# Four plain fp32 weight tiles instead of six, signs partly on ScalarE, quarter steps and a new instruction order in a fused RWKV and MLP kernel

## The chip, the cores and the metric

The kernel runs on one core of a Trainium2 chip. The metric is the device time of one execution in microseconds (us), and for a kernel it is the median of its runs.

The engines are named as in the profile. PE is TensorE's matmul unit and PEld its weight load, DVE is VectorE, ACT is ScalarE, POOL is GpSimd and SP is SyncE. Each engine takes its instructions in the order in which the program lists them for it.

## The reference

An RWKV recurrence over 768 time steps (4 batches, 8 heads of 48) gives `y`. The 3072 tokens of `y` then go through a two-layer MLP: 384 to 2048, an ELU, and back to 384.

```python
for t in range(S):
    kt, vt, rt, wt = (k[:, :, t], v[:, :, t], r[:, :, t], w[:, :, t])
    cur = np.einsum('bhd,bhe->bhde', u[None] * kt, vt)
    y[:, :, t] = np.einsum('bhd,bhde->bhe', rt, state + cur)
    state = wt[:, :, :, None] * state + np.einsum('bhd,bhe->bhde', kt, vt)
...
h = x @ w_in
g = np.where(h > 0.0, h, alpha * (np.exp(np.minimum(h, 0.0)) - 1.0))
return (g @ w_out).astype(np.float32)
```

The two weight matrices arrive as raw 64-bit floats, so the kernel builds fp32 values out of their two 32-bit words by itself.

## The kernel before

**Units and blocks.** The recurrence is cut into 24 units. Four units give the 512 tokens (columns) of one of six blocks. In the first block (block 0) a unit is 128 time steps of one batch, and so a quarter of the block's columns. The steps of a unit have short names:

- `es`, `gs`: two scans of the decays on DVE (L436, L446). `rh` multiplies keys and receptances by them (L451). `rkc` is a product for the diagonal (L470), which PE sums (`pd`, L475), ACT copies (`md`, L479) and ACT, DVE or POOL spreads (`sp`).
- `s`: PE transposes the keys and makes the scores (L516, L528). `mk`: DVE masks them (L540 in block 0, L542 later). `kt`: ACT copies the transposed keys (L546).
- `v`: PE multiplies by the values (L503, L568). `xf`, `xh`, `xl`: ACT and DVE move the result to SBUF, in block 0 as plain fp32 (`xf`), and as a rounded high part and the rest (`xh`, `xl`).

**MLP steps.** A block's MLP goes over 16 weight tiles f of 128 hidden units. One step has the first layer on PE (`g1`, L259 or L263), two activations on ACT (`r1` at L267, `r2` at L270), a combination on DVE (`stt`, L273), a rounding copy on ACT (`gh`, L277), the rest on DVE (`gl`, L281), and the second layer on PE (`g2`, L291 or L294). The result of `g1` lies in one of two PSUM tiles `ph`, which `stt` sets free. The second layer of a block adds up in three PSUM banks `acc`.

In the split form each product is three fp32r matmuls (high by high, high by low, low by high), so a step over 512 columns is 9 matmuls on PE. Six weight tiles (0 to 5) are used in block 0 as plain fp32 (L259, L291): 3 matmuls, each of which the program issues as two passes, and no `gh` and `gl`. In block 0 these six tiles are taken in halves of 256 columns: first the six first halves, which need units 0 and 1 only, then the six second halves. That makes 12 half steps and 10 full steps, numbered 0 to 21.

**Weights.** A tile comes in with one load of 768 KB (`raw`, L606, on SP). ACT scales the high word (`a`, L611), ACT or DVE shifts the low word (`cs`, L616 or L618), DVE joins them (`cb`, L626) and puts the sign in (`cc`, L630). For a split tile ACT then makes the high part (`wh`, L633) and DVE the low one (`wl`, L645). Tiles 0 to 5 are split after block 0 is through with them (`wt` L637 on ACT, `wl` on DVE, `wh` L641 on POOL). There is another branch: ACT writes the sign as a 16-bit float into the low word (`sg`, L622), and then one DVE operation (that of L626) does what `cb` and `cc` do. No tile uses it before the change. Tiles come through four staging buffers at first and two later, so that a later load waits until the `cc` of an earlier tile is done.

**The order.** All these steps are tasks of a planner (`Plan`, L100). It has a table of costs and due times, and plays the schedule through on paper. The instructions are then issued in the order that comes out. `NUDGE` (L87) moves the due times of single tasks by hand, and `FILL` (L45) puts matmuls on ones (L410) ahead of single PE steps. Those compute nothing that is used.

**The end.** In the last block the third bank's columns are finished in two parts (`end`, L303): columns 0 to 383 from PSUM tile `pa`, and columns 384 to 511 from `pb`. Three stores are issued by SP and one, of 128 columns, by ACT.

Of the kernel before, what the change touches and what calls it, by code (L numbers as in the profile page):

```python
# [8 lines left out]
F32 = mybir.dt.float32  # L9
# [11 lines left out]
P = 128  # L21
C = 128
# [5 lines left out]
N = B * C  # L28
# [5 lines left out]
WKR = dict(w=(0, W1), k=(W1, W1 + K1 + R1))  # L34
NU = NC * B
STEP = B // 2
FH = (6, 0)
WU = 64
CUT = 384
K32 = 6  # L40
SIGN_ACT = ()
LOW = ['DVE']*2+['ACT']*14
RAWS = ["raw0", "raw1", "x1a", "x1b"] * 2 + ["raw0", "raw1"] * 4
DUE = {0: 9.0}
FILL = {("pd", 0): 15, ("s", 0): 6, ("v", 0): 1, ("pd", 1): 4, ("v", 1): 1, ("pd", 2): 3, ("s", 2): 2, ("g1", 0): 6}  # L45


def _pieces():
    res = []
    for h in range(H):  # L50
        s, e = h * D, (h + 1) * D
        while s < e:
# [31 lines left out]

LEADS = dict(ld="ld_w ld_k ld_v ld_rk ld_wx", es="es gs", rh="rkc rh kh pc sc", sp="rk rku md pd sp", fl="fl", s="s mk kt", v="v xf xh xl up", raw="raw", a="a",
             cc="cand cs cb cc cx sg", wl="wh wl wt", g1="g1 r1 r2 stt", g2="g2 gh gl")
NUDGE = dict(cc={0: 5, 2: 19.5, 4: 15.75, 5: -13.25, 14: 4.25},  # L87
             es={3: 11.5, 5: -23.75, 7: 1, 11: -42.5, 17: -5.25, 20: 12.75, 21: 40.5},
             g1={16: -3.5, 19: -3.5, 20: 4.25, 23: 5.75, 29: -7.5, 30: -8.25, 31: -13.25, 33: 21, 38: -15.75, 40: -29.75, 42: -33.75, 44: -17.5, 48: -70.75, 51: 26.75, 55: 44, 56: -10.5, 58: -10, 68: 34, 82: -8, 83: 12.5, 84: 6, 93: -7.5},
             g2={2: 6.75, 3: 26.5, 10: 1.5, 19: -1.75, 25: 0.25, 27: 2.25, 30: 0.75, 31: 14.75, 32: -6.5, 35: 9, 37: -11.25, 43: 28.5, 46: -25.25, 51: 8.5, 58: -13, 64: 2.25, 65: 14.5, 71: -25.5, 85: 6.5, 93: 1.75},  # L90
             ld={2: -16, 13: -16.5, 21: -36.75},
             raw={0: -6.75, 1: -6},
             rh={1: 10.25, 4: -3.75, 9: -18.75, 14: 23.5, 16: -14},
             s={4: -29.75, 9: -2.25, 12: -30.25, 13: 5, 21: 8.5},
             sp={4: -19.25, 5: 8.75, 9: 39.5, 13: 29.5, 17: -6.5},
             v={2: -5.5, 15: -2, 17: 6.75, 18: 24, 20: 22.25})
KIND = {n: k for k, v in LEADS.items() for n in v.split()}


class Plan:  # L100
# [5 lines left out]
    def add(self, key, eng, dur, fn, after=(), due=None, start=0.0, lock=False, size=0):  # L106
        self.tasks[key] = dict(key=key, eng=eng, dur=dur, fn=fn, after=list(after), due=due, start=start, lock=lock, size=size,
                               nudge=NUDGE.get(KIND.get(key[0]), {}).get(key[1] if len(key) > 1 else 0, 0.0))

# [124 lines left out]
def mlp(nc, w_h, w_l, ps_acc, ps_h, ml, gp, po, dst, last=False, w_f=()):  # L234
# [61 lines left out]
    box = {}  # L296
# [4 lines left out]
        nc.scalar.copy(box["o"][:, m], acc[m])  # L301

    def end(m, cols=(0, N), rest=None):  # L303
        t = po.tile([P, cols[1] - cols[0]], F32, tag=("wraw", "wraw1", "wg")[m], name="o", bufs=m or 1)
        if rest is not None:
            nc.vector.tensor_tensor(t, rest, box["part"][:, cols[0]:cols[1]], ALU.add)
        else:
            (nc.vector.tensor_copy if m else nc.scalar.copy)(t, acc[m])
        (nc.scalar if cols[1] == N and m == 2 else nc.sync).dma_start(dst[m * P:(m + 1) * P, cols[0]:cols[1]], t)

    def partial():
        box["part"] = gp.tile([P, N], F32, tag="x2", name="part", bufs=1)
# [9 lines left out]
def rwkv_elu_kernel(ctx, tc, wkr, rk, vp, u, uz, gkrw, gv, gu, wraw, out):  # L322
    nc = tc.nc
# [10 lines left out]
    ld = pool("ld", 3)  # L334
# [300 lines left out]
    def conv_t(f):  # L635
        raws[f] = w_f[f], stg.tile([P, 2, NK, P], F32R, tag="wg", name="wt", bufs=SLOTS["wg"])
        nc.scalar.copy(raws[f][1], w_f[f])  # L637
# [24 lines left out]
    add, hold, K = plan.add, plan.hold, COST  # L662
    steps = []
    for c in range(NC):
        fh = FH[c] if c < len(FH) else 0
        fs = list(range(NF)) if c == 0 else list(range(K32, NF)) + list(range(K32))
        steps.append([(f, 0, N // 2) for f in fs[:fh]] + [(f, N // 2, N) for f in fs[:fh]] + [(f, 0, N) for f in fs[fh:]])

    add(("const",), "POOL", 0.5, constants)
    add(("ubd",), "SP", DMA_ISSUE, lambda: load_u(True), due=7.0, size=4.0)  # L670
# [1 line left out]
    for u_ in units:  # L672
        i, c = u_["i"], u_["c"]
# [51 lines left out]
    for f in range(NF):  # L725
        add(("raw", f), "SP", DMA_ISSUE, lambda f=f: load_w(f), start=RAW_AT[min(f, 1)], size=694)
        add(("a", f), "ACT", K["a"], lambda f=f: conv_a(f), [("raw", f)])
        e = LOW[f]
        add(("cs", f), e, K["la" if e == "ACT" else "cand"], lambda f=f: conv_low(f), [("raw", f)], lock=e == "DVE")
        if f in SIGN_ACT:  # L730
            add(("sg", f), "ACT", K["sg"], lambda f=f: conv_sign(f), [("cs", f)])
            add(("cc", f), "DVE", K["cv"], lambda f=f: conv_b(f), [("sg", f), ("a", f)], lock=True)
        else:
            add(("cb", f), "DVE", K["cv"], lambda f=f: conv_b(f), [("cs", f), ("a", f)], lock=True)
            add(("cc", f), "DVE", K["cv"], lambda f=f: conv_c(f), [("cb", f)], lock=True)
        if f >= K32:
            add(("wh", f), "ACT", K["wh"], lambda f=f: conv_h(f), [("cc", f)])
            add(("wl", f), "DVE", K["wl"], lambda f=f: conv_l(f), [("wh", f)], lock=True)
        else:
            add(("wt", f), "ACT", K["wh"], lambda f=f: conv_t(f), [("g2", f), ("g2", f + FH[0])])  # L740
            add(("wl", f), "DVE", K["wl"], lambda f=f: conv_l(f), [("wt", f)], lock=True)
            add(("wh", f), "POOL", K["wg"], lambda f=f: conv_m(f), [("wl", f)], lock=True)
    prior = None
# [4 lines left out]
    for c in range(NC):  # L748
        fns = mlp(nc, w_h, w_l, ps_acc, ps_h, ml, gp, stg, out[:, c * N:(c + 1) * N], last=c == NC - 1, w_f=() if c else w_f)
        t = BEGINS[c]  # L750
# [225 lines left out]
```

## Time and profile before

| | |
|---|---|
| median of 3 runs | 513.03 us (511.89 to 513.47) |
| the profiled execution's own time | 512.88 us |
| its span | 510.8 us |
| PE busy | 498.9 us, 98% of the span |
| DVE busy | 336.5 us, 66% |
| ACT busy | 270.7 us, 53% |
| POOL busy | 94.8 us, 19% |
| HBM read and written | 45.42 MB and 4.72 MB |

A profile row gives an engine, a line, an operation, the tiles written and read, a count, and times. Busy times of PE are modelled and overlap, so what one matmul costs in a stream is the distance between starts. The chain of work that ended last shows that distance: its pieces are start, length and what ran. In the timeline a row is start, length, instruction, and in brackets the idle time just ahead of it with the engine that ended it. "DVE m L273" is `stt`, and "DVE am L542" is `mk`.

### The profile page before, as it was taken

The numbers are of one execution on the slowest core, as the hardware profiler recorded it, in microseconds if no ns is written. First come the engines' busy times: TensorE is split into PE (matmuls) and PEld (weight loads), VectorE is DVE, ScalarE is ACT, GpSimd is POOL, SyncE is SP. The second block draws the span as 40 slices with busy tenths as digits, with TensorE's granted clock in tenths as the row PEclk, the third lists the DMA queues.
The fourth block names the chain that finished last, engine by engine and source line by source line (L and its number), as shares of the span: only waits on it lengthen the run. The fifth ranks groups of instructions, "written<-read, shape, count | busy, mean of one in ns | idle before, by whom it ended". The sixth has DMA issues, their size and how long they took to land.

```text
span 510.8 us, 13742 instructions
## 1 busy us (share of the span) xinstructions
PE 498.9 (98%) x6000; PEld 409.6 (80%) x6000; DVE 336.5 (66%) x469; ACT 270.7 (53%) x520; POOL 94.8 (19%) x94
## 2 busy tenths in 40 slices
PE   8999999999999999999999999999999999999994
PEld 8887778778888888887888888888888877888883
DVE  7999999997799433598633588734499543324232
ACT  4988475757545255565735554343555344534451
POOL 2001124004373100542100271400161100000000
PEclk9999999999999999999999999999999999999998
DMA  8958926302931001944200854204312000000001
GB/s 277 353 192 274 268 93 181 97 4 74 276 91 50 3 1 42 293 137 109 57 3 3 267 161 124 72 1 117 113 50 76 3 3 3 34 27 1 0 2 67
DMA packets 18882, 51.09 MB, mean 100 GB/s; under 512 B 2304, under 2 KB 2688, under 8 KB 18816
## 3 DMA queue, kind: packets, MB, share of 16 engines
q1 hardware_dynamic: 18672, 50.08, 32.2%
q8 instruction: 49, 0.80, 0.7%
q14 instruction: 17, 0.14, 0.1%
q10 hardware_dynamic: 144, 0.07, 0.0%
HBM read 45.42 MB, written 4.72 MB: 98 GB/s over the span
## 4 chain that ended last, share of the span: by engine, by line
PE 84%; DVE 5%; ACT 5%; DMA 3%; issue 1%; DVEq 0%; SPq 0%; ACTq 0%
PE acc L294 35%; PE ph L263 34%; PE pa L503 6%; DMA wraw<-in_wraw_dram 3%; PE pa L528 2%; PE pa L568 2%; PE pb L516 1%; PE ph L259 1%; ACT wraw L616 1%; PE acc L291 1%; DVE wg L626 1%; ACT m L270 1%; PE acc L410 1%; DVE m L273 1%; ACT m L267 1%
## 5 line engine op out<-in xcount | busy, mean ns | idle before, releaser
L273 DVE SCALAR_TENSOR_TENSOR m<-m,ph 128x512 f32<-128x512 f32 (+1 forms) x102 | 66.3, 651 | 96.6 <-ACT m L270 96.4
L267 ACT ACTIVATE m<-ph 128x512 f32<-128x512 f32 (+1 forms) x102 | 58.3, 571 | 108.4 <-PE ph L263 98.0
L263 PE MATMUL ph<-xh,w_l 128*128 128x512 f32 x270 | 105.5, 391 | 0.0
L294 PE MATMUL acc<-gh,w_l 128*128 128x512 f32 x268 | 104.7, 391 | 0.0
L281 DVE TENSOR_TENSOR gl<-m,gh 128x512 fp32r<-128x512 f32 x90 | 64.9, 723 | 38.7 <-ACT gh L277 38.4
L277 ACT CAST gh<-m 128x512 fp32r<-128x512 f32 x90 | 55.7, 619 | 58.4 <-PE acc L294 30.3
L294 PE MATMUL acc<-gh,w_h 128*128 128x512 f32 x180 | 72.0, 400 | 0.0
L263 PE MATMUL ph<-xh,w_h 128*128 128x512 f32 x180 | 71.7, 398 | 0.0
L294 PE MATMUL acc<-gl,w_h 128*128 128x512 f32 x180 | 70.4, 391 | 0.0
L263 PE MATMUL ph<-xl,w_h 128*128 128x512 f32 x180 | 70.2, 390 | 0.0
L270 ACT ACTIVATE m<-m 128x512 f32<-128x512 f32 (+1 forms) x102 | 61.8, 606 | 2.2
L263 PEld LDWEIGHTS ph<-xh,w_l 128*128 128x128 f32 x270 | 50.7, 188 | 10.9
L294 PEld LDWEIGHTS acc<-gh,w_l 128*128 128x128 f32 x268 | 50.3, 188 | 10.6
L496 POOL TENSOR_SCALAR_AFFINE_SELECT am<-md 64x512 f32<-64x512 f32 x32 | 28.9, 903 | 115.6 <-DVE md L465 58.6
L458 POOL TENSOR_TENSOR rk<-rk 128x384 f32<-128x384 f32 x20 | 26.4, 1321 | 120.6 <-DMA rk<-in_rk_dram 120.2
L294 PEld LDWEIGHTS acc<-gh,w_h 128*128 128x128 f32 x180 | 33.8, 188 | 7.8
L263 PEld LDWEIGHTS ph<-xh,w_h 128*128 128x128 f32 x180 | 33.8, 188 | 7.8 <-DVE m L273 0.5
L294 PEld LDWEIGHTS acc<-gl,w_h 128*128 128x128 f32 x180 | 33.8, 188 | 6.8 <-DVE gl L281 0.2
L263 PEld LDWEIGHTS ph<-xl,w_h 128*128 128x128 f32 x180 | 33.8, 188 | 6.7
L263 PE MATMUL ph<-xh,w_g 128*128 128x512 f32 x90 | 36.4, 404 | 0.0
L263 PE MATMUL ph<-xl,w_g 128*128 128x512 f32 x90 | 35.2, 391 | 0.0
L294 PE MATMUL acc<-gh,w_g 128*128 128x512 f32 x88 | 34.9, 397 | 0.0
(116 smaller groups left out, 738.6 us busy)
## 6 DMA issues: line engine op xcount, KB each, us to landing
wraw<-in_wraw_dram SPq DMA_DIRECT2D x16, 768.0 KB, 6.0
k<-in_wkr_dram SPq DMA_DIRECT2D x24, 448.0 KB, 7.0
rk<-in_rk_dram SPq DMA_DIRECT2D x20, 384.0 KB, 4.1
v<-in_vp_dram SPq DMA_DIRECT2D x24, 256.0 KB, 7.3
w<-in_wkr_dram SPq DMA_DIRECT2D x24, 227.9 KB, 4.3
out_dram<-o SPq DMA_DIRECT2D x17, 256.0 KB, 2.1
wx<-in_wkr_dram SPq DMA_DIRECT2D x8, 227.9 KB, 2.9
ub<-in_u_dram SPq DMA_DIRECT2D x1, 192.0 KB, 5.6
```

Of the source, the lines that this page charges most:

```text
L263: nc.tensor.matmul(ph, w[f][:, 0, k], y[:, k], start=(k == n == 0), stop=(k == NK - 1 and n == 2))
L267: act(s["m"], s["ph"], AF.Relu, scale=-1.0)
L270: act(s["m"], s["m"], AF.Exp, scale=-1.0)
L273: stt_(s["m"], s["m"], -1.0, s["ph"], ALU.add, ALU.max)
L277: nc.scalar.copy(s["gh"], s["m"])
L281: nc.vector.tensor_tensor(s["gl"], s["m"], s["gh"].bitcast(F32), ALU.subtract)
L294: nc.tensor.matmul(a_, w[f][:, 1, m], fold(s, g[:, a:b]), start=(first and n == 0), stop=(final and n == 2))
L458: eng.tensor_tensor(u_["rk"][:, 0], u_["rk"][:, 0], u_["rk"][:, 1], ALU.mult)
L496: nc.gpsimd.affine_select(out=am[rs].rearrange("t q p s -> t (q p) s"), in_=u_["md"][rs].rearrange("t q p -> t (q p)").unsqueeze(2).broadc ...
L503: nc.tensor.matmul(u_["py"][32 * j:32 * j + 32, h, k], l, r, **flags)
L528: nc.tensor.matmul(pa[1 - q][ts, p], u_["k"][rs, p, ts], u_["r"][rs, p, ts], start=True, stop=True)
L568: nc.tensor.matmul(u_["pu"][lo:lo + m, h, p], kt[rs, p, lo:lo + m], v[rs, P * p + 80 * z:P * p + 80 * z + D], start=whole, stop=(whole or ...
```

## The change

The change does the following.

1. `FH` and `K32` go from 6 to 4, so tiles 4 and 5 are split tiles from the beginning.
2. `QU = 2`: tiles 0 and 1 take the first half of block 0 in two quarters of 128 columns, so that their first quarter needs unit 0 alone. The steps of block 0 are now 4 quarters, 2 first halves (tiles 2 and 3), 4 second halves and 12 full ones, again numbered 0 to 21.
3. `SIGN_ACT`: for tiles 7, 9, 10, 12, 13 and 15 the sign is written by ACT (`sg`, L627 of the new file), and one DVE operation takes the place of two.
4. `end`: the third bank's two parts go into one tile and leave with one store, and all three stores are issued by ACT.
5. `NUDGE` and `FILL` have new numbers, from which the planner makes another order on every engine. There are 40 fill matmuls instead of 38.

```diff
-FH = (6, 0)
+FH = (4, 0)
...
-K32 = 6
-SIGN_ACT = ()
+K32 = 4
+QU = 2
+SIGN_ACT = (7, 9, 10, 12, 13, 15)
...
-FILL = {("pd", 0): 15, ("s", 0): 6, ("v", 0): 1, ("pd", 1): 4, ("v", 1): 1, ("pd", 2): 3, ("s", 2): 2, ("g1", 0): 6}
+FILL = {("pd", 0): 18, ("s", 0): 6, ("pd", 1): 2, ("s", 2): 3, ("g1", 0): 3, ("g1", 2): 8}
...
-             ld={2: -16, 13: -16.5, 21: -36.75},
+             ld={1: -11.5, 2: 3.75, 16: 17},
...
     def end(m, cols=(0, N), rest=None):
-        t = po.tile([P, cols[1] - cols[0]], F32, tag=("wraw", "wraw1", "wg")[m], name="o", bufs=m or 1)
+        if cols[0] == 0:
+            box[m] = po.tile([P, N], F32, tag=("wraw", "wraw1", "wg")[m], name="o", bufs=m or 1)
+        t = box[m][:, cols[0]:cols[1]]
...
-        (nc.scalar if cols[1] == N and m == 2 else nc.sync).dma_start(dst[m * P:(m + 1) * P, cols[0]:cols[1]], t)
+        if cols[1] == N:
+            nc.scalar.dma_start(dst[m * P:(m + 1) * P], box[m])
...
-        steps.append([(f, 0, N // 2) for f in fs[:fh]] + [(f, N // 2, N) for f in fs[:fh]] + [(f, 0, N) for f in fs[fh:]])
+        head = [(f, j * C, (j + 1) * C) for j in range(2) for f in fs[:QU]] if c == 0 else []
+        steps.append(head + [(f, 0, N // 2) for f in fs[QU if c == 0 else 0:fh]] + [(f, N // 2, N) for f in fs[:fh]] + [(f, 0, N) for f in fs[fh:]])
...
-            add(("wt", f), "ACT", K["wh"], lambda f=f: conv_t(f), [("g2", f), ("g2", f + FH[0])])
+            add(("wt", f), "ACT", K["wh"], lambda f=f: conv_t(f), [("g2", n) for n, x in enumerate(steps[0]) if x[0] == f])
```

Lines of the new file stand two to six higher than those of the old one, depending on the place: L259 is now L261, L291 is L293, L410 is L415.

The first place is PE between the values of unit 1 and those of unit 2. Before, with L410 a fill matmul, L259 a first and L291 a second layer in plain fp32, L516 and L528 the scores of unit 2, L475 the diagonal of unit 3 and L503 the values of unit 2:

```order
L410 MATMUL acc<-ones 128x128 x6
L259 MATMUL ph<-xf,w_f 128x256 x6
L410 MATMUL acc<-ones 128x128 x2
L516 MATMUL pb<-ident,k 128x112 x4
L528 MATMUL pa<-k 128x128 x8
L291 MATMUL acc<-m,w_f 128x2x128 x3
L475 MATMUL pb<-ubd,rkc 128x2 x4
L503 MATMUL pa<-am,v 32x128 x16
```

The same place now, with the new line numbers:

```order
L261 MATMUL ph<-xf,w_f 128x128 x3
L415 MATMUL acc<-ones 128x128 x8
L261 MATMUL ph<-xf,w_f 128x128 x3
L415 MATMUL acc<-ones 128x128 x3
L521 MATMUL pb<-ident,k 128x112 x4
L533 MATMUL pa<-k 128x128 x8
L293 MATMUL acc<-m,w_f 128x2x64 x3
L480 MATMUL pb<-ubd,rkc 128x2 x4
L261 MATMUL ph<-xf,w_f 128x128 x3
L293 MATMUL acc<-m,w_f 128x2x64 x6
L508 MATMUL pa<-am,v 32x128 x16
```

First and second layers of quarters (128 columns) stand where half steps (256 columns) stood. A further quarter of the first layer stands ahead of unit 1's values. The fills are 11 here instead of 8.

The second place is ACT in the middle of block 0. Before, around the high parts of tiles 7 and 8 (L633), with L267 and L270 the two activations of half steps, L616 the shift and L611 the scaling:

```order
L633 CAST w_h<-wg 128x768
L267 ACTIVATE m<-ph 128x256
L270 ACTIVATE m<-m 128x256
L611 ACTIVATE wg<-wraw 128x768
L267 ACTIVATE m<-ph 128x256
L633 CAST w_h<-wg 128x768
L270 ACTIVATE m<-m 128x256
L441 COPY pcs<-eg 112x8
```

Now, around the sign of tile 7 (L627), with L638 the high parts of tiles 5 and 6, and L621 the shift of tile 7:

```order
L638 CAST w_h<-wg 128x768
L621 ACTIVATE wraw<-wraw 128x768
L269 ACTIVATE m<-ph 128x256
L627 ACTIVATE wraw<-wraw 128x768
L272 ACTIVATE m<-m 128x256
L269 ACTIVATE m<-ph 128x256
L638 CAST w_h<-wg 128x768
L272 ACTIVATE m<-m 128x256
```

The sign stands between the two activations of step 6. These belong to the second half of tile 0.

The third place is DVE around the mask of unit 4 (L542, now L547). Before, with L626 the joining of two tiles' words and L281 a `gl`:

```order
L490 TENSOR_TENSOR am<-ident_h,md 128x512
L281 TENSOR_TENSOR gl<-m,gh 128x512 x2
L626 SCALAR_TENSOR_TENSOR wg<-wg,wraw 128x768 x2
L542 COPY_PREDICATED am<-upper_h,pa 128x512
L273 SCALAR_TENSOR_TENSOR m<-m,ph 128x512
```

Now, with L631 the one joining operation of tile 10, L456 a product of unit 5 (`rh`) and L275 an `stt`:

```order
L495 TENSOR_TENSOR am<-ident_h,md 128x512
L631 SCALAR_TENSOR_TENSOR wg<-wg,wraw 128x768
L456 TENSOR_TENSOR k<-k,eg 112x1024
L275 SCALAR_TENSOR_TENSOR m<-m,ph 128x512
L547 COPY_PREDICATED am<-upper_h,pa 128x512
L470 TENSOR_REDUCE md<-rk 128x4x2
```

On PE the values of unit 4 now come one MLP step after its scores, where three steps stood between before. The values of unit 5 come three steps after its scores, where one step stood before.

More of the change, by code (lines that the diff above doesn't have):

```diff
@@ L86 @@
              cc="cand cs cb cc cx sg", wl="wh wl wt", g1="g1 r1 r2 stt", g2="g2 gh gl")
[L87 to L90, printed above, removed]
-             ld={2: -16, 13: -16.5, 21: -36.75},
[L92 to L96, printed above, removed]
+NUDGE = dict(a={11: -10.75, 14: -6.75},
+             cc={3: 27.25, 8: 14.5, 9: -7, 10: -10.5, 12: 10, 14: -13.25, 15: 2},
+             es={3: -46, 9: 32.75, 13: -5.5, 20: -15.25, 21: 30.5},
+             g1={1: 9.25, 2: 9.75, 14: -6.5, 18: 1.75, 30: -1.25, 35: 10, 39: 2.25, 48: 2.25, 53: 15.5, 58: -9, 63: 18.5, 67: 10.25, 78: -4, 79: 7},
+             g2={11: -17, 12: 27, 14: 9.75, 16: 5.25, 32: 9.75, 35: 22.5, 38: 14, 40: -7.75, 41: -7.75, 42: 2.25, 46: 8.5, 47: 8, 51: 23.75, 52: 15, 56: -6, 57: 11.75, 60: 11.75, 61: -18, 63: 5, 68: -5.5, 71: 30.5, 73: 5.25, 77: -16.5, 81: -5.75, 85: 12.25, 87: -4.75, 88: 10.75, 90: 23.75, 94: 21.75},
+             ld={1: -11.5, 2: 3.75, 16: 17},
+             raw={2: 9.5},
+             rh={3: 8, 5: -10, 6: 4.75, 7: 4, 8: 12.5, 12: -19.5},
+             s={2: 14, 15: 14, 17: 9, 23: -34.5},
+             sp={2: 18, 4: -2, 5: -4.5, 6: -5.5, 7: -5.75, 12: -8.75, 20: 3.75},
+             v={2: -8.75, 3: -42.75, 5: 17.25, 20: 9})
 KIND = {n: k for k, v in LEADS.items() for n in v.split()}
```

## The prediction

> **What bounds the kernel now.** I read the page's totals first, then the stages, then who waits for whom.
>
> ```profile
> PE 498.9 (98%) x6000; PEld 409.6 (80%) x6000; DVE 336.5 (66%) x469; ACT 270.7 (53%) x520; POOL 94.8 (19%) x94
> 0.00:10.00 10.00, 8.49 (x54) 8.06 (x54) 7.48 (x14) 3.34 (x10) 3.30 (x14) 1.00 0.83 255
> 30.00:40.00 10.00, 10.00 (x106) 8.20 (x98) 9.97 (x15) 9.75 (x24) 1.08 (x2) 1.00 0.65 224
> 40.00:60.00 20.00, 18.30 (x114) 15.41 (x106) 18.25 (x24) 13.09 (x29) 2.66 (x2) 1.00 0.93 287
> 60.00:80.00 20.00, 19.96 (x149) 16.19 (x149) 19.75 (x26) 13.31 (x24) 5.55 (x4) 1.00 0.31 97
> 80.00:100.00 20.00, 18.95 (x385) 15.29 (x384) 18.95 (x26) 13.72 (x23) 3.52 (x2) 1.00 0.60 177
> 100.00:130.00 30.00, 30.00 (x494) 24.17 (x493) 25.75 (x37) 19.90 (x34) 6.61 (x7) 1.00 0.18 58
> 480.00:500.00 20.00, 20.00 (x90) 16.56 (x89) 7.54 (x12) 9.91 (x18) 0.00 (x0) 1.00 0.01 1
> ```
>
> In a stage's row the columns are its length, the busy time of PE, PEld, DVE, ACT and POOL, then the granted clock, DMA share and GB/s. From 100 us on PE has no idle time to give back. Before 100 us it has a little, and DVE beside it is nearly full: 56.95 of the 60 us from 40 to 100. The clock is 1.00 throughout, so it costs nothing here. All that can change is therefore PE's work, PE's waits in the first 100 us, what PE spends early on fills, and the tail.
>
> The list of PE's waits is short. Here are its three longest but for the start, then the same three in PE's timeline, and two rows of DVE's timeline ahead of the second:
>
> ```profile
> PE ph L259 <- DVE m L273: 1.2, 1, 1.2
> PE pa L503 <- DVE am L542: 1.1, 1, 1.1
> PE acc L291 <- DVE m L273: 0.5, 1, 0.5
> ...
> 49.66 0.70 PE L291 MATMUL acc<-m,w_f 128*128 128x256 f32 x2 [0.55 <-DVE m L273]
> 53.67 1.56 PE L259 MATMUL ph<-xf,w_f 128*128 128x256 f32 x6 [1.15 <-DVE m L273]
> 95.55 0.46 PE L503 MATMUL pa<-k,st 48*32 48x64 f32 x32 [1.05 <-DVE am L542]
> 51.26 2.04 DVE L436 TENSOR_TENSOR_SCAN eg<-w,reset 112x520 f32<-112x520 f32 x1
> 53.23 0.39 DVE L273 SCALAR_TENSOR_TENSOR m<-m,ph 128x256 f32<-128x256 f32 x1
> ```
>
> They add up to 0.55 + 1.15 + 1.05 = 2.75 us. Two of them wait for a `stt`, the third for a mask. The second is a queue effect: its `stt` stood behind a scan of 2.04 us on DVE.
>
> **PE's work.** The chain gives distances between starts in a stream:
>
> ```profile
> 8.11 1.45 PE acc L410 x12
> 55.24 2.59 PE acc L291 x12
> 121.17 2.04 PE acc L294 x9
> ```
>
> Two half steps of a plain tile take 2.59 us on a layer, and one full split step 2.04. Tiles 4 and 5 change from the one to the other on two layers: 4 x (2.59 - 2.04) = **-2.2 us**. That is worth its full price only if PE stays fed (see the rivals).
>
> A quarter has 128 columns a pass, and the trace has no such step. The nearest row is the fill, 1.45 / 12 = 0.121 us a pass, so six passes take 0.73 and two quarters 1.45, against 2.59 / 2 = 1.30 for a half. That happens four times (two tiles, two layers): **+0.6 us**. The ends are 0, if a pass shrinks with its columns, and +1.2, if the first layer of a quarter cannot be packed so closely.
>
> The fills go from 38 to 40 matmuls, 4 passes or 0.5 us more. They stand where PE would wait for DVE or ACT, so I cost them at 0. Without that cover they cost the 0.5.
>
> **The early part, up to the values of unit 3.** Here is where it ends before, and the two DVE operations that matter:
>
> ```profile
> 37.03 1.36 DVE L540 COPY_PREDICATED am<-upper,pa 128x512 f32<-128x512 uint32 x2
> 39.13 0.43 DVE L273 SCALAR_TENSOR_TENSOR m<-m,ph 128x256 f32<-128x256 f32 x1
> 39.47 1.08 PE L503 MATMUL pa<-am,v 128*32 128x128 f32 x32
> 41.08 1.56 PE L259 MATMUL ph<-xf,w_f 128*128 128x256 f32 x6
> ```
>
> DVE is full until this mask ends (37.03 + 1.36 = 38.39). In the new order the same operations stand ahead of it, but four `stt` of a quarter instead of three of a half, which weigh about the same (a half is 0.43). So the mask ends near 38.4 again. PE began these values only at 39.47, since it had a half step to do. It can now begin at 38.4 and be through 1.1 us earlier than 41.08. But by then it has done six half steps' worth of MLP, not eight as before: 2 x 1.30 = 2.6 us less. Of this the quarters' 0.6 is counted already. The rest went into fills and small waits: 2.6 - 1.1 - 0.6 = **+0.9 us**. The ends are 0, if PE's early steps move forward by as much as they lose, and +1.5.
>
> **The waits.** The three old waits stood at places that the new order changes: the scan now stands one step ahead of a step for which PE has other work, and unit 5's values come three steps after its scores. I take all of them as gone: **-2.75 us**. In their place two can come.
>
> The first is behind a sign. A `g1` needs a free `ph`, which `stt` frees, which waits for `r2`, and in the new order `sg` of tile 7 stands ahead of `r2` of step 6. Behind it on ACT are `r1` and `r2` of step 7 and all that follows. The trace shows no sign. The nearest rows are the shift and the scaling on the same engine over as many elements, and far off the slowest elementwise operation of the trace, 1.321 us for 384 elements on POOL:
>
> ```profile
> L616 ACT ACTIVATE wraw<-wraw x8: 905/930/958, 22.1 to 45.2; 128x768 uint32<-128x768 uint32 x8
> L611 ACT ACTIVATE wg<-wraw x5: 909/922/937, 36.5 to 60.0; 128x768 f32<-128x768 f32 x5
> L458 POOL TENSOR_TENSOR rk<-rk 128x384 f32<-128x384 f32 x20 | 26.4, 1321 | 120.6 <-DMA rk<-in_rk_dram 120.2
> ```
>
> So a sign takes between 0.92 and 2 x 1.321 = 2.64 us. At 0.92 PE's next second layer (1.30) hides it. At 2.64 PE waits up to 1.7.
>
> The Trainium skill, page "ScalarE: Activation LUTs", section "What ACT_TABLE_LOAD costs", has an activation cost a fixed part and 0.833 ns an element, whatever the function or type. By that an estimate for 768 elements is 186 + 640 = 826 ns, and the new wait is nothing. The rows above (0.92) agree in size, but no run here shows a 16-bit write.
>
> The second is behind the mask of unit 4, which has one step between scores and values, as unit 5 had before when it waited 1.05. So the new waits lie between 0 and 2.75. I take 0.6 for the sign and 0.4 for the mask, **+1.0** together, nearer the low end, since the rows nearest to a sign are ACT's own.
>
> DVE loses work besides: six signs at 0.87 (41.53 to 42.40 for such an operation and the next):
>
> ```profile
> 41.53 0.96 DVE L630 SCALAR_TENSOR_TENSOR wg<-wraw,wg 128x768 uint32<-128x768 uint32 x1
> 42.40 0.97 DVE L626 SCALAR_TENSOR_TENSOR wg<-wg,wraw 128x768 uint32<-128x768 uint32 x1
> ```
>
> That is 5.2 us, and it gains the splitting of tiles 4 and 5 and two `gl`, some 2.8 us, in the first 60 us rather than after 100. Two POOL copies fall away where PE never waits. All this is worth nothing on its own beyond the waits above.
>
> **The tail.** The last store was issued at 504.18:
>
> ```profile
> 504.18 0.38 ACTq L309 DMA_DIRECT2D out_dram<-o  x1
> ...
> out_dram<-o SPq DMA_DIRECT2D x2, 256.0 KB, 3.0
> out_dram<-o SPq DMA_DIRECT2D x1, 192.0 KB, 2.3
> out_dram<-o ACTq DMA_DIRECT2D x1, 64.0 KB, 3.2
> ```
>
> The last store is now 256 KB at the same place, and the same bytes leave in all. Stores of 64 to 256 KB landed in 2.3 to 3.2 us here, so a change of size is worth between -0.9 and +0.9. I take **+0.2**, for a larger last store behind the same traffic.
>
> **The sum.** -2.2 + 0.6 + 0.9 - 2.75 + 1.0 + 0.2 = -2.25 us. The profiled execution took 512.88 us, 0.15 below the median shown, of which 510.8 was span. So I expect 510.6 us. By the Trainium skill's price for a sign (the page above) the 0.6 would fall away, and the time would be 510.0 us.
>
> **The rivals.**
>
> *Nothing is won, because DVE sets the pace.* If PE is fed by DVE from 40 to 80 us, less work for PE is only longer waits. DVE's 18.25 of 20 and 19.75 of 20 speak for it, and so does the order: `wl` of tiles 4 and 5 and the first `gl` come before most of the signs' relief. Against it speaks that PE itself was at 18.30 and 19.96 there. Then the old waits stay (2.75 not won), 2.8 us of DVE work is added, and the signs of tiles 7 and 9 take off 1.7: -2.2 + 0.6 + 0.9 + 2.8 - 1.7 + 0.2 = +0.6, or 513.5 us.
>
> *Slower, by signs in ACT's queue.* If a sign is near 2.64 us, every one of the six stands in front of some `r1`, `r2` or `gh`, and holds a `ph` for up to 1.7 us. Without any new wait the sum is -3.25. It turns over when a sign costs PE 3.25 / 6 = 0.54 us on average. With half of them hidden behind a second step that PE has ready, the waits are 3 x 1.7 = 5.1, and the time 514.7; with none hidden, 519.8. For it speaks that ACT's order is strict, as this row shows, where ACT waited for a load and moved everything behind it:
>
> ```profile
> 41.78 0.94 ACT L616 ACTIVATE wraw<-wraw 128x768 uint32<-128x768 uint32 x1 [0.68 <-DMA wraw<-in_wraw_dram]
> 42.60 0.48 ACT L591 COPY xf<-pa 128x384 f32<-128x384 f32 x1
> ```
>
> Against it: ACT has a third of its time free from 40 to 100 us. The Trainium skill, page "TensorE: Matmul & The Clock Gate", in its table of specifications, has the queues of ScalarE, VectorE and GpSimdE as strict first in, first out; by that rule the cover of a sign is only what stands ahead, and the trace agrees (the 42.60 above).
>
> *More is won.* No new wait comes and the early part loses nothing: -2.2 + 0.6 - 2.75 + 0.2 = -4.15, or 508.7 us. For it speaks that DVE is relieved by 5.2 us; against it the order of PE's early steps, which is known.
>
> **How the numbers follow.** Forecast 0.50 (509.2 to 511.9 by its open terms), nothing won 0.23, slower by signs 0.10, more won 0.17. A difference of 0.3%, 1.5 us, is about the least that a measurement of this kernel can tell from no change. Faster than that is below 511.5: nearly all of "more" and most of the forecast, 0.17 + 0.43 = 0.60. Within it are the rest of the forecast and nothing won, 0.07 + 0.23 = 0.30. Slower is 0.10. For 8 in 10 the range goes from 508.5 to 513.3. It leaves out the rival by signs and the outer edges of "nothing" and "more".
>
> **What would show it.** Right: the values of unit 3 start near 38.4 us and end near 40. PE's waits between 40 and 100 us sum to about 1.0, and block 0's last second layer ends two to three us earlier than before. A sign is near 0.92 us. After 130 us both traces run in parallel. Wrong: waits of PE on a `stt` behind L627 at more than one sign; waits at the `wl` of tiles 4 to 6; PE gaps after 130 us; or a later start of the values of unit 3, which would say that ACT and not DVE sets the early pace.

## The result and the profile after

| | median us | lowest to highest, runs | ratio to the kernel before [95%] |
|---|---|---|---|
| before, beside it | 512.79 | 511.02 to 514.95, 6 | |
| changed | 518.48 | 518.14 to 518.86, 6 | 1.0115 [1.0094, 1.0136] |

The changed kernel is slower by 1.15%, or 5.7 us. The forecast was 510.6 us with a range up to 513.3, so it had the wrong sign. The profiled execution took 518.76 us, with a span of 516.8 (before 510.8). In the experiments a ratio is to the kernel before, timed beside the run (medians of 511.4 to 512.06 us), and leaves out executions over 1.5% above the fastest of their kernel; medians and ranges are of all.

The stages come first, in the columns of the prediction's table (length, PE, PEld, DVE, ACT, POOL, granted clock, DMA share, GB/s). This is the changed kernel:

```profile
0.00:10.00 10.00, 6.39 (x36) 6.20 (x36) 7.13 (x14) 1.68 (x3) 3.31 (x14) 1.00 0.76 204
10.00:20.00 10.00, 9.94 (x89) 8.98 (x91) 7.36 (x10) 5.76 (x19) 0.00 (x0) 0.62 1.04 308
20.00:30.00 10.00, 10.00 (x115) 9.14 (x114) 6.02 (x9) 6.82 (x19) 0.00 (x0) 0.70 1.03 281
30.00:40.00 10.00, 9.80 (x126) 9.02 (x124) 9.96 (x15) 9.16 (x28) 1.08 (x2) 1.00 0.42 145
40.00:60.00 20.00, 19.48 (x148) 15.89 (x144) 17.93 (x26) 19.97 (x36) 1.01 (x1) 1.00 0.80 241
```

The kernel before, from 10 to 30 us:

```profile
10.00:20.00 10.00, 10.00 (x165) 8.87 (x165) 9.84 (x15) 8.46 (x25) 0.00 (x0) 1.00 1.03 362
20.00:30.00 10.00, 9.43 (x97) 8.41 (x96) 9.76 (x14) 8.60 (x20) 0.00 (x0) 1.00 0.79 252
```

Two things stand there that the kernel before did not have. PE is idle for 3.6 of the first 10 us (1.5 before). And from 10 to 30 us the granted clock is 0.62 and 0.70. PE reads as busy there (9.94 and 10.00), but takes longer for the same matmuls, and DVE, which the prediction took as full, has 7.36 and 6.02.

PE's timeline shows how it begins. Before, the diagonal of unit 0 (L475) and its scores (L528) stood here:

```profile
7.05 1.05 PE L475 MATMUL pb<-ubd,rkc 112*128 112x2 f32 x8 [0.43 <-DVE rkc L470]
...
10.05 1.16 PE L528 MATMUL pa<-k 48*128 48x128 f32 x16
```

Now the fills (L415) end, and the diagonal of unit 0 (L480) waits:

```profile
1.07 6.39 PE L415 MATMUL acc<-ones 128*128 128x128 f32 x36 [1.07 <-POOL ones L382]
10.06 1.02 PE L480 MATMUL pb<-ubd,rkc 112*128 112x2 f32 x8 [2.60 <-DMA ubd<-in_uz_dram]
...
13.26 2.08 PE L533 MATMUL pa<-k 48*128 48x128 f32 x16
```

The releaser is a load of 3.5 KB. In the list of DMA issues its last number is the time from issue to landing. Here is the row of the kernel before, then that of the changed one:

```profile
ubd<-in_uz_dram SPq DMA_DIRECT2D x1, 3.5 KB, 3.9
ubd<-in_uz_dram SPq DMA_DIRECT2D x1, 3.5 KB, 7.2
```

In the kernel before, the load was third on SP and issued at 1.74 us; in the changed one it was issued at 2.67. There it is fifth, behind 2 loads of `w` and 2 of `k`. The scores of unit 0 (L533) take 2.08 us where they took 1.16. What follows on DVE are the masks of units 0, 1 and 3 (before: 11.36, 17.01 and 37.03):

```profile
15.49 1.34 DVE L545 COPY_PREDICATED am<-upper,pa 128x512 f32<-128x512 uint32 x2 [1.96 <-PE pa L533]
...
23.95 1.34 DVE L545 COPY_PREDICATED am<-upper,acc 128x512 f32<-128x512 uint32 x2 [4.34 <-PE acc L533]
...
43.48 1.35 DVE L545 COPY_PREDICATED am<-upper,pa 128x512 f32<-128x512 uint32 x2
```

DVE stood still for 1.96 + 4.34 = 6.30 us because of PE, and the values of unit 3 start at 45.26 us instead of 39.47.

The list of PE's waits (total, times, longest) has, besides that load:

```profile
PE ph L265 <- DVE m L275: 2.1, 2, 1.4
...
PE ph L261 <- DVE m L275: 0.5, 1, 0.5
PE acc L296 <- DVE gl L283: 0.4, 1, 0.4
```

The longest of them, 1.43 us at 149.95, is a `stt` that stands behind a scan on DVE:

```profile
147.26 2.06 DVE L441 TENSOR_TENSOR_SCAN eg<-w,reset 112x520 f32<-112x520 f32 x1
149.24 1.25 DVE L275 SCALAR_TENSOR_TENSOR m<-m,ph 128x512 f32<-128x512 f32 x2
```

At the end the change won time. From the start of the last DVE operation (503.85 before, 512.54 after) to the end of the span it was 6.95 us and is now 4.26. The records of SP's own queue at the kernel's last branch show what moved. First the kernel before, where SP has three of the last stores:

```profile
L853 SPq EVENT_SEMAPHORE  x8: 17/17/17, 508.9 to 509.5; - x8
L853 SPq COMPARE_BRANCH  x1: 45/45/45, 505.3 to 505.3; - x1
```

And the changed kernel, where it has none:

```profile
L859 SPq EVENT_SEMAPHORE  x8: 17/17/17, 456.2 to 515.5; - x8
L859 SPq COMPARE_BRANCH  x1: 45/45/45, 453.7 to 453.7; - x1
```

Before, SP's branch stood behind its stores at 505.3, and its next record came 3.6 us later. Afterwards that branch stands at 453.7, 63 us ahead of the end of the span.

So the 6.0 us of span divide up like this. Up to the start of the values of unit 3: 45.26 - 39.47 = +5.8. From there to the last DVE operation: 467.28 against 464.38, or +2.9. The tail: 4.26 - 6.95 = -2.7.

This is the account of one execution. Of the six of the changed kernel it has the lowest granted clock on the mean of its span, 0.987; the other five have 0.992 to 0.997. All six took between 518.1 and 518.9 us, so over these executions the time does not follow the clock.

### The profile page after: what moved, and what is told of

It is laid out like the page before. It is cut to its first block, busy times and chain, and to the rows that moved or that the text cites. A ratio compares the mean times of both kernels' runs of the same rounds, so it can differ in the third digit from the quotient of the medians.

```text
span 516.8 us, 13782 instructions
## 1 busy us (share of the span) xinstructions
PE 504.7 (98%) x6016; PEld 413.4 (80%) x6016; DVE 328.8 (64%) x465; ACT 280.9 (54%) x528; POOL 93.0 (18%) x92
## 4 chain that ended last, share of the span: by engine, by line
PE 78%; DVE 9%; ACT 5%; DMA 4%; issue 3%; SPq 0%; DVEq 0%; ACTq 0%
PE ph L265 32%; PE acc L296 32%; PE pa L508 5%; PE pa L533 2%; DMA wraw<-in_wraw_dram 2%; PE pa L573 2%; DVE eg L441 1%; PE pb L521 1%; DMA ubd<-in_uz_dram 1%; DVE m L275 1%; DVE k L456 1%; DVE gl L283 1%; PE acc L293 1%; ACT m L272 1%; ACT m L269 1%
## 5 line engine op out<-in xcount | busy, mean ns | idle before, releaser
L275 DVE SCALAR_TENSOR_TENSOR m<-m,ph 128x512 f32<-128x512 f32 (+2 forms) x102 | 65.9, 649 | 97.9 <-ACT m L272 97.8
L269 ACT ACTIVATE m<-ph 128x512 f32<-128x512 f32 (+2 forms) x102 | 58.6, 575 | 94.7 <-PE ph L265 84.9
L265 PE MATMUL ph<-xh,w_h 128*128 128x512 f32 x216 | 86.1, 398 | 2.5 <-DVE m L275 2.1
L296 PE MATMUL acc<-gh,w_h 128*128 128x512 f32 x216 | 86.7, 401 | 0.0
L296 PE MATMUL acc<-gl,w_h 128*128 128x512 f32 x216 | 84.4, 391 | 0.4 <-DVE gl L283 0.4
L265 PE MATMUL ph<-xl,w_h 128*128 128x512 f32 x216 | 84.1, 389 | 0.0
L272 ACT ACTIVATE m<-m 128x512 f32<-128x512 f32 (+2 forms) x102 | 62.0, 609 | 2.1
L296 PEld LDWEIGHTS acc<-gl,w_h 128*128 128x128 f32 x216 | 40.6, 188 | 8.8 <-DVE gl L283 1.1
L441 DVE TENSOR_TENSOR_SCAN eg<-w,reset 112x520 f32<-112x520 f32 (+1 forms) x24 | 32.2, 1351 | 1.4 <-DMA w<-in_wkr_dram 1.4
L451 DVE TENSOR_TENSOR_SCAN eg<-w,reset 112x520 f32<-112x520 f32 (+1 forms) x24 | 32.4, 1352 | 0.8
L456 DVE TENSOR_TENSOR k<-k,eg 112x1024 f32<-112x1024 f32 x24 | 32.1, 1337 | 0.0
```

Source lines behind the costliest of these rows:

```text
L265: nc.tensor.matmul(ph, w[f][:, 0, k], y[:, k], start=(k == n == 0), stop=(k == NK - 1 and n == 2))
L269: act(s["m"], s["ph"], AF.Relu, scale=-1.0)
L272: act(s["m"], s["m"], AF.Exp, scale=-1.0)
L275: stt_(s["m"], s["m"], -1.0, s["ph"], ALU.add, ALU.max)
L296: nc.tensor.matmul(a_, w[f][:, 1, m], fold(s, g[:, a:b]), start=(first and n == 0), stop=(final and n == 2))
L441: nc.vector.tensor_tensor_scan(out=eg[:, 0, 0:n][:, ::-1], data0=u_["w"][:, 1:n + 1][:, ::-1], data1=reset[:, 0, 0:n][:, ::-1], initial=0. ...
```

## The experiments

The theory (A): the new order of loads delays `ubd`, PE idles ahead of the first diagonal, and this costs twice, by late scores and by the clock, which falls after the idle time and makes the next 10 to 20 us of PE slow. Rivals: (B) signs of 1.94 us in a nearly full ACT (19.97 of 20 from 40 to 60 us) set the pace; (C) quarters and four plain tiles leave PE too little to do early.

Where an edit moves tasks, it reorders the list that the planner returns (`todo`), so that nothing else moves.

**1. ubd second.** The changed kernel, and:

```diff
-        for t in plan.order():
+        todo = plan.order()
+        todo.insert(2, todo.pop(5))
+        for t in todo:
```

> The changed kernel with the small load of ubd issued second on SP, right behind the first load of w, not fifth; nothing else moves. Theory A (the late ubd costs the time): PE's diagonal of unit 0 waits for rkc, 8.47 us, and no longer for ubd, 10.06. The granted clock stays 1.00 from 10 to 30 us, the 6.3 us in which DVE waited for scores shrink to under 1, the mask of unit 3 starts near 37.5 us instead of 43.48, and the time falls by 5 to 6 us, to 512.5 to 513.5. Theory B (signs of 1.9 us in a full ACT set the early pace): the mask of unit 3 comes at most 1.5 us earlier, and the time stays over 517. Theory C (quarters and four plain tiles leave PE too little early work): PE idles or fills longer early, the time stays over 517 although the masks are early.

Measured: median 516.49 us (511.58 to 520.65, 10 executions), ratio 1.0074 [1.0045, 1.0102]. The profiled execution took 512.32:

```profile
8.90 1.05 PE L480 MATMUL pb<-ubd,rkc 112*128 112x2 f32 x8 [1.09 <-DVE rkc L475]
```

In this execution the clock was 1.00 throughout, the mask of unit 3 started at 37.80, and the time was 6.4 us below that of the changed kernel's profiled execution, as theory A has it. But the median fell by only 2, and the times lay 9 us apart. The gap had gone from 2.60 to 1.09 us, and something was left to chance. The clock has a part in that: the two slowest executions (519.58 and 520.65) have mean clocks of 0.991 and 0.988. But it is not all of it, since seven executions with 0.997 and more lie between 511.58 and 517.86.

**2. The kernel before with the changed kernel's first loads.** `todo` is sorted so that it begins with these tasks, and keeps its order behind them:

```diff
+        head = [("const",), ("ld_w", 0), ("ld_w", 1), ("ld_k", 0), ("ld_k", 1), ("ubd",)]
```

> The kernel before, with SP's first loads in the order of the changed one (w of units 0 and 1, k of units 0 and 1, then ubd, then the first weight tile); nothing else moves. Theory A: ubd lands near 10 us, PE waits 2 to 3 us for it, the clock falls between 10 and 30 us, and the kernel before gets the loss: 4 to 6 us, to 517 to 519. If only the lateness of the first scores counts and not the clock, 2 to 3 us. Theories B and C: at most 1 us slower, since neither signs nor quarters are in it.

Measured: 516.27 us (515.08 to 517.65), ratio 1.0079 [1.0056, 1.0102]. The kernel before gets most of the loss by the loads alone, without signs, quarters or a new order elsewhere. Its first diagonal and its second ten microseconds:

```profile
10.06 1.84 PE L475 MATMUL pb<-ubd,rkc 112*128 112x2 f32 x8 [3.24 <-DMA ubd<-in_uz_dram]
```

```profile
10.00:20.00 10.00, 9.94 (x95) 9.26 (x97) 5.95 (x9) 5.37 (x17) 0.00 (x0) 0.71 1.03 322
```

That speaks against B and C as the main cause.

**3. More fills, ubd as late as before.** The changed kernel with

```diff
-FILL = {("pd", 0): 18, ...
+FILL = {("pd", 0): 29, ...
```

> The changed kernel with 29 fill matmuls ahead of the first diagonal instead of 18, so that PE has work until ubd lands near 10 us; ubd is as late as before. Theory A with the clock as its cause (the gap of 2.6 us lowers the clock, and the slow PE makes the masks late): the clock is 1.00 from 10 to 30 us, the scores of unit 0 take 1.16 us and not 2.08, the mask of unit 1 starts near 19 us instead of 23.95, and the time falls to 512.5 to 514.5. Theory A with the lateness as its cause: the first diagonal is at 10 us as it was, and the time stays at 517 to 518.5. Theories B and C: 518.5, no change.

Measured: 514.20 us (513.12 to 515.15), ratio 1.0053 [1.0034, 1.0072]. These fills compute nothing, `ubd` is no earlier (the diagonal is at 10.14), and yet the loss is more than halved. The second ten microseconds have their clock back:

```profile
10.00:20.00 10.00, 9.41 (x125) 8.45 (x126) 7.94 (x11) 7.53 (x23) 0.00 (x0) 1.00 1.03 302
```

So filling the idle time wins 4.3 of the 5.7 us with `ubd` as late as before, and in the profiled executions the clock comes back with it. How much of the 4.3 us is the clock's is not shown: three executions of the changed kernel with a mean clock of 0.997, by which PE lost at most 1.8 us of work to it (0.35% of the span), took as long as the profiled one. The lateness remains: the mask of unit 3 starts at 39.41, 2.4 us later than in the kernel before.

**4. Signs on DVE.** The changed kernel, in its order, with

```diff
-... add(("sg", f), "ACT", K["sg"], lambda f=f: conv_sign(f), ...
+... add(("sg", f), "ACT", K["sg"], lambda: None, ...
-... lambda f=f: conv_b(f), [("sg", f), ...
+... lambda f=f: (conv_b(f), conv_c(f)), [("sg", f), ...
```

> The changed kernel, in the changed order, with the six signs made by DVE in place of ACT: ACT's step for the sign is empty, and the join's place on DVE holds both DVE operations. Theory B (six signs of 1.94 us on ACT cost PE time): 2 us or more are won, to 516.5 or less. Theory A: the signs are beside the cause; DVE has 5.2 us more between 50 and 107 us, ACT 11.6 less, and the time stays within 1.5 us of 518.5, or rises if DVE is the tighter of the two.

Measured: 518.31 us (515.57 to 522.95), ratio 1.0134 [1.0067, 1.0201]: nothing is won without the signs on ACT. That speaks against rival B, though DVE does their work instead. The price itself was mixed with the clock here, so run 8 repeats it on a cleaner base.

**5. ubd second, and 24 fills.** Run 1 with `("pd", 0): 24`.

> The changed kernel with ubd issued second and 24 fill matmuls ahead of the first diagonal, so that PE has no gap there (with 18 it had one of 1.09 us, and the times were scattered from 511.6 to 520.7). Theory A, the clock falls after a gap in PE's early work: no gap over 0.4 us before 20 us, clock 1.00 from 10 us on, a median of 511 to 512.5, and a scatter under 2 us in all. Rival, the scatter comes from something else, as the loads: it stays 4 us or more wide, with a median over 514.

Measured: 513.46 us (512.45 to 514.44, 12 executions), ratio 1.0032 [1.0017, 1.0047]. Six fills more than in run 1 took 3 us from the median and brought the range from 9 us down to 2. The median is a little above what was expected; the gap was still 0.70 in the profiled execution.

**6. A gap without a late ubd.** Run 1 with `("pd", 0): 12`.

> The changed kernel with ubd issued second, so that it is in time, and 12 fill matmuls ahead of the first diagonal, not 18: PE idles for about 2.4 us as in the changed kernel, but the first diagonal stands at 8.9 us and not at 10.06. Theory A with the clock: a granted clock below 0.9 in 10 to 20 or 20 to 30 us, slow scores or values of unit 0 or 1, and 516 to 519. Theory A with the lateness of ubd alone: clock or not, DVE is not kept waiting for more than 1 us, and the time is 511.5 to 513.5.

Measured: 516.98 us (516.13 to 518.89), ratio 1.0116 [1.0084, 1.0149]. The first diagonal stood at 9.56, against 9.59 in the profile of run 5, so its data were no later, but PE had idled for 3.60 us before it, more than was meant:

```profile
10.00:20.00 10.00, 9.89 (x105) 9.02 (x105) 7.76 (x11) 6.16 (x19) 0.00 (x0) 0.73 1.04 316
```

The gap alone costs 3.5 us against run 5. The mean clock is 0.989 to 0.993 in its four executions, and 0.994 to 1.000 in the twelve of run 5.

**7. The kernel before with all four last stores on ACT.**

```diff
-        (nc.scalar if cols[1] == N and m == 2 else nc.sync).dma_start(...)
+        nc.scalar.dma_start(...)
```

> The kernel before, with all four last stores issued by ACT, so that SP has none; the four pieces stay. In the changed kernel SP's last branch (45 ns, then 2.5 us until its next record) comes at 453.7 us and the span ends 4.0 us after the last DVE operation; in the kernel before that branch comes behind SP's last store, at 505.3, its next record is 3.6 us later, and the span ends 6.7 us after the last DVE operation. Theory D (SP's branch behind its stores is what the tail saved): 2.3 to 2.9 us faster than the kernel before, near 509.2. Rival (one store of 256 KB in place of two parts saved it): no change within 0.5 us, or slower, since four issues of 0.8 us stand in a row on ACT.

Measured: 511.62 us (508.43 to 514.86, 12 executions), ratio 1.0000 [0.9977, 1.0024]. In the profile SP's branch did move away from the end:

```profile
L853 SPq EVENT_SEMAPHORE  x8: 17/17/17, 507.6 to 508.1; - x8
L853 SPq COMPARE_BRANCH  x1: 45/45/45, 447.1 to 447.1; - x1
```

The tail there was 5.71 us, 1.24 less than before, and the span 509.5. The median did not follow. The times lay 6.4 us apart, which no idle time of PE in this profile explains. The branch alone is not shown to be worth anything in the time. Nor is the tail a clear sign: with the old end and the branch behind SP's stores it was 6.95 us in the kernel before, 6.58 in run 2 and 5.68 in run 12.

**8. Signs on DVE, on the base of run 5.** The edit of run 4.

> The kernel with ubd second and 24 fills, and the six signs made by DVE (ACT's step is empty, the join's place holds both DVE operations). Without a gap at the start the price of the signs is not mixed with the clock. By the first run with signs on DVE, whose work behind the mask of unit 3 took 3.7 us longer: 514.5 to 516, that is 3 to 4 us slower than the same kernel with the signs on ACT. If that run's loss was the clock's: within 1 us of it.

Measured: 516.25 us (515.53 to 517.79), ratio 1.0096 [1.0071, 1.0122], 2.8 us over run 5. In this order the signs on ACT are a gain.

**9. The kernel before with the whole new end.** `end` of the changed kernel, and nothing else.

> The kernel before with the whole new end and nothing else: the third bank in one tile and one store, all three last stores issued by ACT. With ACT issuing four stores the span ended 5.7 us after the start of the last DVE operation, where the kernel before has 6.95 and the changed kernel 4.3. Theory D2 (the branch of SP is worth 1.2 us and the fewer stores the rest): the span ends 4.2 to 5.2 us after that start, 2 to 2.7 us are won, 509 to 510. Rival (the end's gain doesn't reach the time, as the run with four stores on ACT had the median of the kernel before): 511.2 to 512.

Measured: 509.13 us (508.15 to 510.31, 11 executions), ratio 0.9955 [0.9941, 0.9969]. The tail was 4.14 us. This is the one part of the change that is shown to win by itself, and this kernel is the fastest of all that were run.

**10. The changed kernel with the old start.** `todo` is sorted so that it begins with the first loads of the kernel before and its DVE steps of unit 0, with 15 fills ahead of the first diagonal:

```diff
+        head = [("const",), ("ld_w", 0), ("ld_k", 0), ("ubd",), ("ld_w", 1), ("raw", 0), ("ld_k", 1),
+                ("es", 0), ("gs", 0), ("rkc", 0), ("es", 1), ("pd", 0), ("rh", 0)]
```

> The changed kernel with the start of the kernel before: SP loads w and k of unit 0 and ubd first, DVE makes both scans and rkc of unit 0 ahead of the first scan of unit 1, and 15 fills stand ahead of the first diagonal. All else is the changed order. Theory A: the first diagonal is near 7.1 us, the clock 1.00, the values of unit 3 start 1 to 2 us earlier than the 40.4 of the kernel with ubd second and 24 fills, and the time is 511 to 512.5, 1 to 2 us below that kernel's 513.5. Rival (DVE is full from 10 to 40 us whatever the start): values of unit 3 at 40 and 513.5 as before.

Measured: 516.80 us (513.94 to 519.29, 6 executions), ratio 1.0114 [1.0088, 1.0140]. The expectation failed. The first diagonal came at 7.11 and the values of unit 3 at 38.91, as expected, and still the time rose against run 5. The stage shows why that could be:

```profile
10.00:20.00 10.00, 8.78 (x130) 7.77 (x132) 9.31 (x14) 8.31 (x24) 0.00 (x0) 1.00 1.03 352
```

PE has less to do there than in any other kernel so far, with waits of 0.46 and 0.77 us ahead of the second diagonal and the first values. In this execution, the fastest of the six, the clock held (0.999 on the mean of the span). In the others the mean is 0.996 (515.55 us) and 0.988 to 0.993 (516.10 to 519.29), so in the four slowest at least it fell. Runs 13 and 14 were made for that.

**11. The same with a scan moved.** On DVE the first scan of unit 9 goes behind the two `stt` that PE waited for at 149.95.

```diff
+        todo.insert(spot("pc", 9), todo.pop(spot("stt", 27)))
+        todo.insert(spot("pc", 9) - 1, todo.pop(spot("es", 9)))
```

> The same, and on DVE the first scan of unit 9 behind the combinations of MLP steps 26 and 27, not ahead of them: PE waited 1.42 us for them near 144 us in every kernel with the changed order. Theory: this wait goes, nothing else comes in its place, and 1.4 us are won against the kernel with the old start alone. Rival: the scan's own users are then late and the wait comes back at the next scores or values: under 0.5 us won.

Measured: 514.85 us (512.08 to 519.65, 8 executions), ratio 1.0075 [1.0042, 1.0107]. The wait of 1.43 us went, and one of 0.69 for the mask of a later unit came a few us after it. Half of it was won at the place; in the median the spread hides it. The profiled execution had a clock of 0.83 from 10 to 20 us.

**12. Old start and old end.** Run 10 with `end` of the kernel before.

> The changed kernel with the old start and also the old end (third bank in two tiles and two stores, three of four stores issued by SP). By the tails of the traces (4.2 to 5.2 us with the new end, 6.6 to 7.0 with the old) it is 1.5 to 2.7 us slower than the kernel with the old start and the new end. Rival: within 0.5 us of it.

Measured: 516.77 us (515.32 to 521.59, 6 executions), ratio 1.0113 [1.0074, 1.0151], the same as run 10. The tail was 5.68 against 4.58 us, but both kernels are spread over 5 us, so this run tells nothing about the end. It does show chance at work: the idle pieces of PE were 0.34, 0.43 and 0.79 us, nearly those of run 10 (0.18, 0.46 and 0.77), and here the clock fell:

```profile
10.00:20.00 10.00, 8.78 (x102) 7.59 (x103) 7.80 (x12) 7.71 (x20) 0.00 (x0) 0.76 1.03 356
```

**13. The idle pieces filled.** Run 11 with

```diff
-FILL = {("pd", 0): 15, ("s", 0): 6, ("pd", 1): 2, ("s", 2): 3, ...
+FILL = {("pd", 0): 17, ("s", 0): 6, ("pd", 1): 4, ("v", 0): 4, ("s", 2): 6, ...
```

> The changed kernel with the old start and the moved scan, and more fills where PE idled in it: 17 instead of 15 ahead of the first diagonal, 4 instead of 2 ahead of the second, 4 instead of none ahead of the values of unit 0, 6 instead of 3 ahead of the scores of unit 2. The kernel without them had PE at 8.78 of 10 us from 10 to 20 and times from 512.1 to 519.7. Theory A (idle time of PE in the first 25 us, even in pieces under 1 us, lowers the clock in some executions): PE over 9.7 there, times within 2.5 us of each other, a median of 511 to 512.5. Rival (the scatter has another cause): times still spread over 5 us or more, a median over 513.5.

Measured: 511.36 us (509.75 to 513.26, 12 executions), ratio 0.9988 [0.9974, 1.0003]. Eleven matmuls on ones, which nothing reads, took 3.5 us from the median and brought the range from 7.6 to 3.5 us, where 2.5 was expected. The mean clock is 0.997 to 1.000 in all twelve executions. PE is now full early:

```profile
10.00:20.00 10.00, 9.99 (x135) 8.89 (x136) 9.15 (x14) 8.28 (x22) 0.00 (x0) 1.00 1.03 342
```

**14. A gap by which nothing can be late.** Run 9 without the 6 fills ahead of the first scores:

```diff
-FILL = {("pd", 0): 15, ("s", 0): 6, ("v", 0): 1, ...
+FILL = {("pd", 0): 15, ("v", 0): 1, ...
```

> The kernel before with the new end (509.1 us, all its times within 2.2 us), and without the 6 fill matmuls ahead of the scores of unit 0. Nothing waits for a fill, so no step can be later by this; PE only idles for about 1.6 us from 8 to 9.6. Theory A: in some executions the clock falls after it, the times spread over 4 us or more and the median rises by 1.5 us or more. Rival (only late data costs time): no change within 0.5 us and a scatter of about 2 us as before.

Measured: 513.59 us (510.75 to 517.36, 12 executions), ratio 1.0032 [1.0010, 1.0054], against 0.9955 with the fills. No step needs a fill, and 4 us are lost in the median. The profiled execution was the slowest of the twelve:

```profile
7.30 1.05 PE L478 MATMUL pb<-ubd,rkc 112*128 112x2 f32 x8 [1.25 <-DVE rkc L473]
9.76 0.57 PE L519 MATMUL pb<-ident,k 112*128 112x112 f32 x4 [1.41 <-DVE reset L448]
```

```profile
10.00:20.00 10.00, 10.00 (x92) 8.56 (x92) 7.16 (x10) 5.92 (x19) 0.00 (x0) 0.54 1.03 366
20.00:30.00 10.00, 10.00 (x94) 8.99 (x95) 6.42 (x9) 6.29 (x16) 0.00 (x0) 0.61 0.77 241
```

Here are the same low DVE and the same low clock as in the changed kernel, out of idle pieces of 1.25 and 1.41 us. Only the second stands where fills were left out. The first comes from the 30 passes of the other fills, which took 4.97 us in this execution and 5.86 in that of run 9. And DVE waits again for the scores of unit 1:

```profile
22.01 1.34 DVE L543 COPY_PREDICATED am<-upper,acc 128x512 f32<-128x512 uint32 x2 [4.23 <-PE acc L531]
```

So idle time of PE at the start costs some 4 us although nothing waits for a fill. That it does so by the clock is seen in the profile and over the twelve executions: the mean clock is 0.993 in the two fastest (510.75 and 511.60) and 0.981 to 0.983 in the three slowest (516.26 to 517.36). In run 9 it is 0.997 to 1.000.

## Why the prediction was wrong, point by point

**The early part** is the step that failed. It was priced at +0.9 us on the premise that DVE is full until the mask of unit 3 ends and that the same operations stand ahead of it. The operations on DVE ahead of that mask were the ones that it named. What was left out is what DVE waits for. The prediction didn't follow SP's queue, past which `ubd` had been moved, up to the first step of PE that needs it. It measured +5.8 us in place of +0.9 in the profiled execution. Runs 2, 3 and 6 show both halves: the late load, and the idle time with the clock that falls after it. The prediction did name a later start of these values as a sign of being wrong, but would have put it down to ACT.

**The clock** was read as 1.00 throughout and dismissed ("it costs nothing here"). That held for the kernel before, which had no idle piece over 0.43 us between its first matmul and 20 us. A condition of the old profile was taken for a property of the chip.

**The fills** were costed at 0, or 0.5 without cover. That counted only their own duration. Runs 3, 13 and 14 show another use: with 6 to 11 of them the clock holds in the profiled executions, and without them 3 to 4.5 us go.

**PE's work, -2.2 us**, was too large. The direction was right: eight half steps of 1.31 us went and four full ones came. But all full steps together took 9.5 us more in the changed kernel and 8.8 in run 13, where four at 2.04 are 8.2 (distances between starts, summed over the steps after the values of unit 3, without idle time). The prediction took the 2.04 from a stretch without other work. A step next to the recurrence's matmuls takes longer, 2.26 beside 2.05 in the changed kernel's chain:

```profile
115.71 2.26 PE acc L296 x9
117.98 2.05 PE ph L265 x9
```

So -1.0 to -1.7 us. Whether the four new steps are the dear ones is not shown; the kernel before has steps of 2.27 us too. By the prediction's prices PE's work in the stretch from the values of unit 3 on changes by 4 x 2.04 - 6 x 1.30 = +0.4 (two fewer half steps fall ahead of it, so it loses only six), and it measured +2.0. The quarters were priced rightly: at full clock six passes take 0.67 to 0.78 us, forecast 0.73.

**The waits.** The three old ones went, as forecast (-2.75). The new ones are 3.7 us after 40 us in the changed kernel, not 1.0. The one behind a sign is there with 0.52 us, forecast 0.6. The sign stands ahead of `r2` (L272) on ACT, and PE has the wait:

```profile
50.37 1.94 ACT L627 ACTIVATE wraw<-wraw 128x768 f16<-128x768 f32 x1
52.03 0.48 ACT L272 ACTIVATE m<-m 128x256 f32<-128x256 f32 x1
```

```profile
53.03 1.56 PE L261 MATMUL ph<-xf,w_f 128*128 128x256 f32 x6 [0.52 <-DVE m L275]
```

A second sign, at 87.39, stands ahead of a tile's high part, for which PE waits 0.22 us, and then 0.26 for its low part. The wait for the mask of unit 4 did not come. The two largest new ones, 1.43 us at 149.95 and 0.70 at 76.29, stand behind scans on DVE: they are of the same kind as one of the old waits that the prediction had just removed, and the first lies after 130 us, where it had both traces in parallel. The rival "slower, by signs" did not come true. A sign costs 1.94 us, inside its bounds and nearer the upper one, but with the signs on DVE the kernel is slower by 2.8 us (runs 5 and 8).

**The tail, +0.2 us** with ends of 0.9 either way, measured -2.7 in the profile, and -2.3 in the time when done alone (run 9). The prediction weighed the sizes of stores. What the change also did is to move the stores to another queue and to leave out one issue. Run 9 shows what the new end is worth as a whole. How that divides between the queue and the fourth store is not shown, since run 7 won nothing in the time.

**What is left open.** With the start repaired (run 13) the changed kernel is level with the kernel before, although it has the new end, which alone wins 2.3 us. So its other parts cost about 1.7 us even with the clock held. In the profiles the stretch from the values of unit 3 to the last DVE operation is 3.0 us longer in run 13 than in run 9 (465.96 and 463.00), and these values start 0.4 us earlier. Dearer full steps and other waits are in that, but no run separates four plain tiles, quarters and the new order. Also open are the spreads of runs 1 and 7, and why the changed kernel's executions with a mean clock of 0.997 were no faster than the one with 0.987.

## What to carry to other kernels

When an order changes, follow every load that moved to the first instruction that waits for it, the smallest ones above all: the changed order of the first loads alone cost the kernel before 0.8%, and PE's first long wait was for one of 3.5 KB. Idle time at the start can cost more than its own length, through the clock of what comes after, so filler on PE has a value that its busy time doesn't show. A price taken from an undisturbed stretch of a stream was too low here for the same step beside other work.

## What the runs showed of the hardware

In these profiles the granted clock is either 1.00 or 0.50; values between are means over a stretch. It fell to 0.50 after PE had idled for 2.60 us (changed kernel), 3.24 (run 2) and 3.60 (run 6), after 1.25 and 1.41 us with 1 us of work between them (run 14), and after pieces of 0.34 to 1.01 us (runs 11 and 12). In run 4 it fell 6 us after a gap of 2.45 us had ended. It held in the profiled executions with 1.09 (run 1), 0.94 (run 3) and 0.70 us (run 5), and with the pieces of run 10, so chance has a part in it. It stayed at 0.50 for 3.4 us in runs 4 and 11, 6.8 in runs 2, 6 and 12, 13.7 in the changed kernel and 17.1 in run 14, though PE read as busy for 9.9 to 10.0 of 10 us in the last two and in runs 2 and 6. The Trainium skill, page "TensorE: Matmul & The Clock Gate", section "What's actually happening", has the clock halved after an idle window of some 3.4 us and the windows running free of the program, so that the moment differs from run to run. That runs 10 and 12 differ agrees with the free windows. The measured gaps of 2.60, and of 1.25 and 1.41, are shorter than its window. The page has the full clock back after some 3.4 us of sustained work: runs 4 and 11 agree, and the other five took two to five times as long. Where they differ, the measurement decides.

A sign on ACT, 768 elements from 32 to 16 bits, took 1928 to 1973 ns, twice the shift over as many elements (884 to 978 ns). The Trainium skill's price, page "ScalarE: Activation LUTs", section "What ACT_TABLE_LOAD costs", by which the prediction worked out an estimate of 826 ns, does not hold for it. The page gives that price for every function in fp32 and bf16, which the prediction took for every type; the sign is written as f16.

A load of 3.5 KB took 7.2 us to land behind four loads of 228 to 448 KB on the same queue, 3.9 us behind two (the kernel before) and 2.5 behind one (run 1).
